# Kept sums stored by token tile, output channels regrouped for 2 KB reloads, and the second V weight quarter on ScalarE's DMA queue

## The chip, the cores and the metric

One core of one Trainium2 chip. The metric is device time in microseconds (us), and the granted clock of TensorE is 1.0 for nearly every run.

Engines in the profile: PE is TensorE's matmul part, PEld its weight loads, DVE VectorE, ACT ScalarE, POOL GpSimd, SP SyncE (which issues nearly all DMAs).

## The reference, cut to what matters

Two transformer-like layers, each an attention part A and a gated feed-forward part B, over 2048 tokens of 1024 channels. The attention looks at 8 earlier tokens at a distance of 2 (0, 2, ... 14 back), in 32 heads of 32 channels.

```python
def _A_ref(x, wqkv, wo):                 # H = 32, Dh = 32, W = 8, dil = 2
    q, k, v = ...(x @ wqkv)
    logits = einsum("bhsd,bhswd->bhsw", q, k at s - 2*w) * Dh**-0.5
    o = einsum("bhsw,bhswd->bhsd", softmax(logits, -1), v at s - 2*w)
    return o.reshape(B, S, D) @ wo
x = x + _A_ref(_layernorm(x), ...);  x = x + _B_ref(_layernorm(x), ...)   # twice
```

## The kernel before

The kernel works on blocks of 512 tokens (BLK), four tiles of 128 (TPB) each; two layers of four blocks make the numbers n = 0 to 7. VectorE multiplies q by the shifted k and sums over channel groups. What remains is S: 128 partitions (32 heads x 4 partial sums) by 8 window places by 512 tokens. S goes to DRAM and comes back with heads and token tiles on the partitions, for the softmax. (Block 0 alone sums over the heads' partitions with TensorE instead.) The attention output O goes to DRAM and comes back channel by channel as the stationary operand of the Wo matmul.

```python
s_d = [dram.tile([P, W, BLK], BF16, name=f"s_d{i}") for i in range(2)]
...
def store_s(n, half): ...
    sp_dma(s_d[n % 2][:, ws, :], att[n]["s"][:, ws, :])          # 4 KB runs
def load_s(n): ...
    for tq in range(TPB):
        src = bass.AP(tensor=sd.tensor, offset=sd.offset + tq * P,
                      ap=[[DG * W * BLK, H], [BLK, DG * W], [1, P]])   # 256-byte runs
        sp_dma(s4[32 * tq:32 * tq + 32, :, :, :].rearrange("p d w t -> p (d w) t"), src)
def load_o(n): ...
    for tq in range(TPB):
        src = bass.AP(..., ap=[[P, P], [P * P, KC], [1, P]])           # 256-byte runs
        sp_dma(oTa[:, :, tq, :], src)
```

The start is a hand-made pipeline. While the inputs arrive, 13 "scratch" matmuls on ones keep TensorE busy. x tile 0 is normalized by VectorE (`bn`, `aggr`, `apply`) with a power on GpSimd, transposed by TensorE, copied out of PSUM by ScalarE and VectorE, and multiplied by the first half of V's weights. Tile 1 follows. Its eight transposes (`turn`) are done in two groups of four, which lie in one PSUM tile.

```python
def load_x(b, tiles): ...   # tile 0: half on SyncE's queue, half on ScalarE's; tile 2: ScalarE's queue
load_x(0, range(TPB - 1)); ...
load_slab(("v0", 0), ...)   # V weights, quarters 1 and 2, both on SyncE's queue
load_x(0, [TPB - 1])
load_slab(("v0", 1), ...)   # quarters 3 and 4
load_slab(("qk01", "q", 0), ...)
...
scratch(13)
bn(0, 0); bn(0, 1); aggr(0)
act_square(2); act_mean(2)              # ScalarE, before its copies of tile 0
bn(1, 0); apply(0, 0); apply(0, 1); turn(0)
copy(0, "a", 0, 0, KC // 4); copy(0, "a", 0, KC // 4, KC // 2)
...
both = psum_l.tile([P, 2, KC, P], BF16, tag="L", name="tp_pair")   # tile 1: one PSUM tile
tps[t] = [both[:, h, 0:KC // 2, :] for h in range(2)]
...
def second(h): turn(1, (h,)); copy(1, "v", h); ...
def head():
    for kc in range(KC // 2):
        if kc == KC // 2 - 1: ln["second"](0)     # after 24 matmuls of tile 0
        for c in range(KC): prod(kc, c, 0, 1)
    ln["second"](1)
```

## Time and profile before

| | before |
|---|---|
| time, median of 3 | 1618.2 us (1617.9 to 1618.39) |
| span of the profiled run | 1616.4 us |
| PE busy | 1611.3 us |
| first V matmul / steady V products of tile 1 / first Q projection (chain) | 8.09 / 10.80 / 24.04 us |

From the page of the kernel before: busy time and share of PE, DMA packets by size, and two of the DMA issues (KB each, median us from issue to landing).

```profile
PE 1611.3 (100%) x7633; PEld 786.6 (49%) x7633; DVE 1137.1 (70%) x960; ACT 475.8 (29%) x968; POOL 180.4 (11%) x168
...
DMA packets 407448, 317.92 MB, mean 197 GB/s; under 512 B 166464, under 2 KB 387008, under 8 KB 406848
...
w_o<-in_A_wo_dram SPq DMA_DIRECT2D x16, 1024.0 KB, 7.0
oT<-o_d SPq DMA_DIRECT2D x32, 256.0 KB, 4.5
```

The S reloads from the list of DMAs:

```profile
s<-s_d SPq DMA_DIRECT2D x28, 256.0 KB, 6.1
```

All that PE ever waited for (total us, times, longest us):

```profile
PE scratch L132 <- DVE ones L310: 1.5, 1, 1.5
PE acc_v L132 <- ACT xnT_first L328: 0.4, 1, 0.4
```

The chain of work that ended last, at its start (start us, duration us, what):

```profile
5.45 1.16 ACT xn_first L328 x2
6.63 1.15 ACT xn_first L328 x2
7.78 0.27 ACT xnT_first L328
8.09 1.50 PE acc_v L132 x24
9.59 0.33 PE tp_pair L385 x4
9.94 0.43 DVE xnT_first L106
10.42 0.38 PE tp_pair L385 x4
10.80 3.53 PE acc_v L132 x48
...
24.04 2.16 PE acc_q L132 x10
```

How to read it: a DMA's landing is the moment at which its completion is seen, and the chain is followed back from the last instruction, at each step to what released it. A slab is a part of a weight matrix loaded by one call. PE waits 1.5 us for its first operand and 0.4 us for the first transposed copy, and never again. From 24.04 us on the chain is matmul after matmul, eight of 128x512 in 1.727 us. About 7332 of these, 56 half-wide ones and the 8 head-sum matmuls of block 0 (0.55 us) add up to 1582.6 + 6.1 + 0.55 = 1589.3 us, which is the whole way to the last matmul near 1613.3 us. Only the 24 us at the start can change, as long as nothing new makes PE wait later. In the chain the first matmul (8.09) hangs on ScalarE's copy, which stands behind the square and mean of x tile 2 (5.45 to 7.78).

### The profile page before, as it was taken

How to read it: one execution, taken by the hardware profiler on the slowest of the kernel's cores; microseconds unless marked ns; L12 is line 12 of the kernel's file. 1: busy time of each engine (PE TensorE's matmuls, PEld its weight loads, DVE VectorE, ACT ScalarE, POOL GpSimd, SP SyncE). 2: the span in 40 equal slices, each digit the busy share in tenths (PEclk: the TensorE clock that was granted, in tenths of full speed). 3: DMA queues.
4: the chain of work that ended last, by engine and by line, in shares of the span. 5: the costliest groups of instructions: out<-in, count | busy, mean ns of one | idle time of the engine just before them, and what ended most of it. 6: DMA issues, size and time to landing. Idle time of an engine off the chain costs nothing.

```text
span 1616.4 us, 18930 instructions
## 1 busy us (share of the span) xinstructions
PE 1611.3 (100%) x7633; PEld 786.6 (49%) x7633; DVE 1137.1 (70%) x960; ACT 475.8 (29%) x968; POOL 180.4 (11%) x168
## 2 busy tenths in 40 slices
PE   9999999999999999999999999999999999999999
PEld 6646544444444445444454444544445444444444
DVE  5999989996989698929489293893939939311211
ACT  5853312132116313603136031361313311131110
POOL 2400100010003002300053000530005100000000
PEclk9999999999999999999999999999999999999999
DMA  9868868697669766794847947479574794755452
GB/s 306 180 190 238 224 159 262 183 216 204 208 192 217 200 184 212 192 246 146 227 160 201 240 153 230 152 205 252 165 226 155 203 245 157 209 161 177 157 167 68
DMA packets 407448, 317.92 MB, mean 197 GB/s; under 512 B 166464, under 2 KB 387008, under 8 KB 406848
## 3 DMA queue, kind: packets, MB, share of 16 engines
q1 hardware_dynamic: 406784, 316.13, 69.9%
q8 instruction: 59, 0.97, 0.3%
q10 hardware_dynamic: 576, 0.59, 0.1%
q14 instruction: 29, 0.24, 0.0%
HBM read 266.29 MB, written 34.66 MB: 186 GB/s over the span
## 4 chain that ended last, share of the span: by engine, by line
PE 99%; DMA 0%; ACT 0%; DVE 0%; issue 0%; ACTq 0%; DVEq 0%
PE acc_u L132 24%; PE acc_g L132 24%; PE dacc L132 18%; PE acc_v L132 7%; PE acc_wo L132 7%; PE acc_k L132 7%; PE acc_q L132 7%; PE dacc_pair L132 6%; DMA x<-in_A_x_dram 0%; ACT xn_first L328 0%; PE tp_pair L385 0%; PE L L132 0%; DVE x L837 0%; DVE xnT_first L106 0%; ACTq L175 0%
## 5 line engine op out<-in xcount | busy, mean ns | idle before, releaser
L132 PE MATMUL acc_g<-xnT_b,w_g 128*128 128x512 bf16 x1792 | 423.3, 379 | 0.0
L132 PE MATMUL acc_u<-xnT_b,w_u 128*128 128x512 bf16 x1792 | 423.3, 379 | 0.0
L790 ACT ACTIVATE r<-acc_g 128x512 bf16<-128x512 f32 x224 | 133.5, 596 | 726.7 <-PE acc_g L132 701.6
L106 DVE TENSOR_TENSOR hT<-acc_u,r 128x512 bf16<-128x512 f32 x224 | 150.5, 685 | 240.7 <-PE acc_u L132 238.2
L132 PE MATMUL dacc<-w_d,hT 128*128 128x512 bf16 (+1 forms) x1400 | 301.9, 375 | 0.0
L132 PEld LDWEIGHTS <-hT 128*128 128x128 bf16 x1820 | 178.1, 98 | 208.9
L132 PEld LDWEIGHTS <-w_u 128*128 128x128 bf16 x1792 | 175.3, 98 | 211.5
L132 PEld LDWEIGHTS <-w_g 128*128 128x128 bf16 x1792 | 175.4, 98 | 211.4
L106 DVE TENSOR_TENSOR pv<-a,vhm 128x4096 bf16<-128x4096 bf16 x64 | 143.4, 2281 | 0.0
L837 DVE TENSOR_TENSOR x<-dacc,x 128x512 bf16<-128x512 f32 (+1 forms) x38 | 24.5, 672 | 154.2 <-PE dacc L132 154.2
L608 DVE TENSOR_TENSOR t<-q,k 128x2048 f32<-128x2048 bf16 x56 | 128.0, 2292 | 6.7 <-ACT k L543 4.6
L106 DVE TENSOR_TENSOR t<-q,k 128x2048 f32<-128x2048 bf16 x56 | 127.4, 2285 | 3.7 <-ACT k L543 2.6
L106 DVE TENSOR_TENSOR pv<-pv 128x1024 bf16<-128x1024 bf16 (+1 forms) x128 | 113.6, 947 | 0.0
L549 POOL COPY kh<-k 128x14 bf16<-128x14 bf16 x40 | 56.0, 1406 | 504.3 <-ACT k L543 504.3
L132 PE MATMUL acc_wo<-w_o,oT 128*128 128x512 bf16 x512 | 111.8, 379 | 0.0
L621 DVE TENSOR_TENSOR ac<-ac,t 128x2048 f32<-128x2048 f32 x48 | 109.6, 2284 | 0.3
L106 DVE TENSOR_TENSOR ac<-ac,t 128x2048 f32<-128x2048 f32 x48 | 109.5, 2282 | 0.0
L264 POOL TENSOR_TENSOR st_b<-st_b,neg_half 128x1 f32<-128x1 f32 x29 | 43.9, 1523 | 525.8 <-ACT st_b L263 525.7
L132 PE MATMUL dacc_pair<-w_d,hT 128*128 128x512 bf16 x420 | 95.9, 379 | 0.0
L132 PEld LDWEIGHTS <-oT 128*128 128x128 bf16 x512 | 50.0, 98 | 60.4
L259 ACT ACTIVATE xn_b<-x 128x1024 bf16<-128x1024 bf16 x29 | 30.3, 1045 | 129.1 <-DVE x L106 67.0
L446 ACT CAST vT<-acc_v 128x512 bf16<-128x512 f32 x56 | 32.8, 588 | 57.6 <-PE acc_v L132 56.6
(134 smaller groups left out, 1230.0 us busy)
## 6 DMA issues: line engine op xcount, KB each, us to landing
w_g<-in_B_W_gate_dram SPq DMA_DIRECT2D x56, 1024.0 KB, 7.4
w_u<-in_B_W_up_dram SPq DMA_DIRECT2D x56, 1024.0 KB, 5.5
w_d<-in_B_W_down_dram SPq DMA_DIRECT2D x48, 1024.0 KB, 5.7
w_o<-in_A_wo_dram SPq DMA_DIRECT2D x16, 1024.0 KB, 7.0
vhm<-v_d SPq DMA_DIRECT2D x32, 284.0 KB, 6.8
v_d<-vT SPq DMA_DIRECT2D x8, 1024.0 KB, 9.8
oT<-o_d SPq DMA_DIRECT2D x32, 256.0 KB, 4.5
w_d<-in_B_W_down_dram SPq DMA_DIRECT2D x16, 512.0 KB, 3.9
```

The lines of the kernel that those rows point to most:

```text
L106: tail_dve[0] = f(*args, **kwargs).ins
L132: tail_pe[0] = nc.tensor.matmul(*args, **kwargs).ins
L259: nc.scalar.activation(xn, xt[:], ACT.Square, accum_out=sq)
L264: nc.gpsimd.tensor_tensor(rstd, vpe, neg_half[:, 0:1], op=ALU.pow)
L446: tail_act[0] = nc.scalar.copy(st["vT"][:, c, :], acc[:]).ins
L549: nc.gpsimd.tensor_copy(khalo[n][:, c, :], k[:, BLK:BLK + HALO])
L608: nc.vector.tensor_tensor(t[:], i0, i1, op=ALU.mult)
L621: nc.vector.tensor_tensor(o, ac[:], t[:], op=ALU.add)
L790: tail_act[0] = nc.scalar.activation(rs[j][:], acc[:], ACT.Relu).ins
L837: run = dv if n < NB - 2 else (lambda f, *args, **kwargs: f(*args, **kwargs))
```

## The change

Intent: S is kept by token tile, so that a reload takes 2 KB runs; O is reloaded with eight neighbouring channels per partition, also in 2 KB runs, and Wo's rows are regrouped to match. At the start, ScalarE's copies come before its work on tile 2, tile 3's statistics move to VectorE, tile 1's first transposes come four matmuls later, and V's second weight quarter goes to ScalarE's DMA queue in place of x tile 2.

```diff
-    wo_v = A_wo.rearrange("(kc p) n -> p kc n", p=P)
+    wo_v = A_wo.rearrange("(p kc) n -> p kc n", kc=KC)
-    s_d = [dram.tile([P, W, BLK], BF16, name=f"s_d{i}") for i in range(2)]
+    s_d = [dram.tile([P, TPB, W, P], BF16, name=f"s_d{i}") for i in range(2)]
-            elif t == 2:
-                nc.scalar.dma_start(x_tiles[t][:], x_dram[t * P:(t + 1) * P, :])
-    load_x(0, range(TPB - 1))
+    load_x(0, [0, 1])
-                sp_dma(tv[:, rows, :], src[:, rows, :])
+                start = nc.scalar.dma_start if (key[1], i) == (0, 1) else sp_dma
+                start(tv[:, rows, :], src[:, rows, :])
-    load_x(0, [TPB - 1])
+    load_x(0, [2, 3])
-        act_square(2)
-        act_mean(2)
         bn(1, 0)
         ...
         copy(0, "a", 0, KC // 4, KC // 2)
+        act_square(2)
+        act_mean(2)
         ...                       # tile 3: bn and aggr on VectorE, after tile 1's copies
-                if kc == KC // 2 - 1:
-                    ln["second"](0)
                 for c in range(KC):
+                    if (kc, c) == (KC // 2 - 1, KC // 2):
+                        ln["second"](0)
-                       rhs=st["s"][:, WH * wh:WH * (wh + 1), tq * P:(tq + 1) * P],
+                       rhs=st["s"][:, tq, WH * wh:WH * (wh + 1), :],
-            o = st["s"][:, WH * h:WH * (h + 1), :] if c == KC - 1 else ac[:]
+            if c == KC - 1:
+                o = _ap(st["s"], WH * h * P, [[P, WH], [W * P, TPB], [1, P]])
-                              ap=[[DG * W * BLK, H], [BLK, DG * W], [1, P]])
+                              ap=[[DG * W * BLK, H], [W * BLK, DG], [1, W * P]])
-                              ap=[[P, P], [P * P, KC], [1, P]])
-                sp_dma(oTa[:, :, tq, :], src)
+                              ap=[[KC * P, P], [1, KC * P]])
+                sp_dma(oTa[:, tq, :, :].rearrange("p c t -> p (c t)"), src)
 ... (shapes and slices that follow from these left out)
```

More of the change, by code (lines that the diff above doesn't have):

```diff
@@ L408, in ln_first @@
         copy(0, "v", 1)
-        act_power(2)
         apply(1, 0)
@@ L414, in second @@
             turn(1, (h,))
+            copy(1, "v", h)
             if h == 0:
-                copy(1, "v", 0)
                 return
-            copy(1, "v", 1)
+            bn(3, 0)
+            act_power(2)
+            bn(3, 1)
+            aggr(3)
             apply(2)
-            act_square(3)
-            act_mean(3)
-            act_power(3)
             apply(3)
@@ L596, in f @@
                 if h == 0 and c == 0:
-                    st["s"] = big_tile([P, W, BLK], f"s_{n}")
+                    st["s"] = big_tile([P, TPB, W, P], f"s_{n}")
                 i0, i1 = qk_bcast(n, c, WH * h, WH)
@@ L616, in add @@
             ac, t = st["ac"], st.pop(("t", c))
-            o = st["s"][:, WH * h:WH * (h + 1), :] if c == KC - 1 else ac[:]
+            o, i0, i1 = ac[:], ac[:], t[:]
+            if c == KC - 1:
+                o = _ap(st["s"], WH * h * P, [[P, WH], [W * P, TPB], [1, P]])
+                i0, i1 = (i[:].rearrange("p w (q t) -> p w q t", t=P) for i in (ac, t))
             if n < NB:
-                dv(nc.vector.tensor_tensor, o, ac[:], t[:], op=ALU.add)
+                dv(nc.vector.tensor_tensor, o, i0, i1, op=ALU.add)
             else:
-                nc.vector.tensor_tensor(o, ac[:], t[:], op=ALU.add)
+                nc.vector.tensor_tensor(o, i0, i1, op=ALU.add)
         return [mult(h, c) for h in range(2) for c in range(KC)]
@@ L627, in f @@
             ws = slice(WH * half, WH * (half + 1))
-            sp_dma(s_d[n % 2][:, ws, :], att[n]["s"][:, ws, :])
+            sp_dma(s_d[n % 2][:, :, ws, :], att[n]["s"][:, :, ws, :])
         return f
@@ L635, in f @@
             for tq in range(TPB):
-                src = bass.AP(tensor=sd.tensor, offset=sd.offset + tq * P,
-                              ap=[[DG * W * BLK, H], [BLK, DG * W], [1, P]])
-                sp_dma(s4[32 * tq:32 * tq + 32, :, :, :].rearrange("p d w t -> p (d w) t"), src)
+                src = bass.AP(tensor=sd.tensor, offset=sd.offset + tq * W * P,
+                              ap=[[DG * W * BLK, H], [W * BLK, DG], [1, W * P]])
+                sp_dma(s4[32 * tq:32 * tq + 32, :, :, :].rearrange("p d w t -> p d (w t)"), src)
             att[n]["s4"] = s4
@@ L733, in f @@
             b = n % NB
-            oTa = big_tile([P, KC, TPB, P], f"oT_{n}")
+            oTa = big_tile([P, TPB, KC, P], f"oT_{n}")
             for tq in range(TPB):
                 src = bass.AP(tensor=o_d.tensor, offset=o_d[b * TPB + tq:b * TPB + tq + 1].offset,
-                              ap=[[P, P], [P * P, KC], [1, P]])
-                sp_dma(oTa[:, :, tq, :], src)
+                              ap=[[KC * P, P], [1, KC * P]])
+                sp_dma(oTa[:, tq, :, :].rearrange("p c t -> p (c t)"), src)
             att[n]["oT"] = oTa
@@ L755, in f @@
                         for c in range(KC):
-                            mm(accs[t, half][:], lhsT=st["oT"][:, c, t, :], rhs=slab[("o", n, half)][:, c, :],
+                            mm(accs[t, half][:], lhsT=st["oT"][:, t, c, :], rhs=slab[("o", n, half)][:, c, :],
                                start=(c == 0), stop=(c == KC - 1))
```

## The prediction

> **What bounds the kernel.** TensorE, almost without a gap. The page shows PE busy 1611.3 of 1616.4 us at granted clock 1.0. The Trainium skill, "Trainium Kernel Development and Optimization" (Performance Expectations), calls matmul busy time a bad metric because matmuls are pipelined, so I counted. In the chain of waits eight 128x512 matmuls take 1.727 us everywhere (216 ns each). From 24.04 us, where the first Q projection starts, to the last matmul near 1613.3 us there are about 7332 such matmuls, 56 half-wide ones and the 8 head-sum matmuls (0.55 us): 1582.6 + 6.1 + 0.55 = 1589.3 us, the whole stretch. No PE time is lost there. The list of PE waits agrees: 1.5 us for the ones tile and 0.4 us for the first transposed copy, nothing else. Only the first 24 and last 3 us can change, and the diff does not touch the tail.
>
> **Regrouping S and O.** Each S reload (28 issues of 256 KB, median 6.1 us to landing) and O reload (32 of 256 KB, 4.5 us) is cut into 256-byte runs. 4096 packets per block become 512: of 407448 packets about 48,000 go (25,000 for S, 29,000 for O, less 5,000 more on the S store, which goes from 4 KB to 1 KB runs). I expect landings roughly halved (estimate, from about 280 GB/s in the slices of an O reload against 380 to 400 in the 2 KB weight loads at the start). What waits for these: VectorE 2.2 us in all for S; PE never for O. Off the path, worth 0. Wo's rows are permuted to match, still 1 KB runs. The last add of S gets a four-level pattern; fp32 adds take 2.28 to 2.29 us whatever their layout (broadcast and shifted forms alike), so I expect 2.29 us still. It must: S of block 0 ends at 102.65 us and its head-sum matmuls run at 103.4.
>
> **The start.** Before: x tile 0 lands near 4.0 us; statistics, power and apply end near 6.9; transposes 6.97 to 7.69. ScalarE's copy waits behind square and mean of tile 2 (5.45 to 7.78), so the first V matmul starts at 8.09. After, the copies go first: start about 7.45, first matmul about 7.8, a gain of 0.3 us. But the next link eats it: tile 1's apply ends its first half at 9.41 (GpSimd power to 9.01), and 28 matmuls, four transposes, VectorE copy, four transposes give 7.8 + 28 x 0.0625 = 9.55, then about 0.9 us to the second transposes, about 10.4, against 10.42 before. The steady run begins at 10.8 in both. Risk: V's first quarter now shares bandwidth with the second one on ScalarE's queue; at the measured 390 GB/s[...] it lands near 7.5 instead of 6.8, just in time. Tiles 2 and 3 land near 8.2 and 8.8; apply of 2 ends near 13.2, of 3 near 14.7, before their transposes (14.2, 17.3).
>
> **Time.** 1618.2 - 0.1 = 1618.1 us, 8 in 10 within 1617.5 to 1618.6. Faster by over 2%: 0.003; within 2%: 0.994; slower: 0.003.
>
> **What would show it.** First V matmul near 7.8 us; first product of tile 1 near 10.8; Q projection near 24.0; the chain from there unchanged within 0.1 us; packets near 359,000; S and O landings near half; S add 2.29 us.
>
> **What would make it wrong.** V's quarter landing after 7.8 us; a slower patterned S add stalling the head sums at 103 us; tile 2's apply coming after 14.2 us; an O or S load colliding with a weight load so that PE waits.

## The result, and the profile after

| | before | after |
|---|---|---|
| time, median of 6 | 1618.42 us (1617.9 to 1619.06) | 1618.22 us (1618.09 to 1618.59) |
| span of the profiled run | 1616.4 us | 1616.1 us |
| chain: first V matmul / tile 1 steady / first Q | 8.09 / 10.80 / 24.04 | 7.55 / 10.52 / 23.76 us |
| DMA packets; of these under 512 B | 407,448; 166,464 | 359,064; 105,024 |

The ratio is 0.9999, 95% interval 0.9986 to 1.0012: the same. (Ratios are the mean time of one kernel's fast runs over that of the other's in the same rounds, so not quite the ratio of the medians quoted.)

The lines that answer to those of before. Page of the changed kernel:

```profile
PE 1607.6 (99%) x7584; PEld 786.4 (49%) x7633; DVE 1138.5 (70%) x962; ACT 473.5 (29%) x964; POOL 180.3 (11%) x168
...
DMA packets 359064, 317.92 MB, mean 197 GB/s; under 512 B 105024, under 2 KB 332736, under 8 KB 358464
...
w_o<-in_A_wo_dram SPq DMA_DIRECT2D x16, 1024.0 KB, 8.2
oT<-o_d SPq DMA_DIRECT2D x32, 256.0 KB, 3.4
```

PE's smaller busy time is no gain: the trace has 7584 of the 7633 matmul records, some are missing. The S reloads:

```profile
s<-s_d SPq DMA_DIRECT2D x28, 256.0 KB, 6.1
```

PE's waits:

```profile
PE scratch L132 <- DVE ones L309: 1.5, 1, 1.5
PE tp L384 <- DVE xn_first L106: 0.8, 1, 0.8
PE tp_pair L384 <- DVE xnT_first L106: 0.3, 1, 0.3
```

The start of the chain:

```profile
0.81 2.89 DMA x<-in_A_x_dram
...
6.24 0.41 DVE xn_first L106
6.69 0.41 PE tp L384 x4
7.13 0.38 ACT xnT_first L327
7.55 1.72 PE acc_v L132 x28
9.27 0.36 PE tp_pair L384 x4
9.66 0.44 DVE xnT_first L106
10.13 0.38 PE tp_pair L384 x4
10.52 3.53 PE acc_v L132 x48
...
23.76 2.37 PE acc_q L132 x11
```

Three things stand out. The DMA side changed as intended: 48,384 packets fewer, and the O reload lands in 3.4 us instead of 4.5. But the S reload takes 6.1 us as before, and Wo's loads take 8.2 us instead of 7.0. And the whole start sits 0.28 us earlier (10.52 against 10.80; 23.76 against 24.04). It is tempting to call this 0.28 us the gain of the new start. x tile 0 landed earlier by just that much, though: VectorE's first statistics began at 3.72 us against 4.00. Did the change do that?

My theory: the landing of x tile 0 is chance, and the new order gains nothing because the next link, tile 1's transposes, takes the gain. Rivals: the new queues bring tile 0 in earlier; the new order brings the 0.28 us; or the regrouping helps somewhere later. For the reloads, my theory was that they have slack everywhere.

### The profile page after: what moved, and what is told of

It reads as the page before. It is cut to its first block, busy times and chain, and to the rows that moved or that the text cites. A ratio compares the mean times of both kernels' runs of the same rounds, so it can differ in the third digit from the quotient of the medians.

```text
span 1616.1 us, 18879 instructions
## 1 busy us (share of the span) xinstructions
PE 1607.6 (99%) x7584; PEld 786.4 (49%) x7633; DVE 1138.5 (70%) x962; ACT 473.5 (29%) x964; POOL 180.3 (11%) x168
## 2 busy tenths in 40 slices
DMA packets 359064, 317.92 MB, mean 197 GB/s; under 512 B 105024, under 2 KB 332736, under 8 KB 358464
## 4 chain that ended last, share of the span: by engine, by line
PE 99%; issue 0%; DMA 0%; DVE 0%; POOL 0%; ACT 0%; DVEq 0%
PE acc_u L132 24%; PE acc_g L132 24%; PE dacc L132 18%; PE acc_v L132 7%; PE acc_k L132 7%; PE acc_q L132 7%; PE acc_wo L132 7%; PE dacc_pair L132 6%; DMA x<-in_A_x_dram 0%; PE tp_pair L384 0%; DVE bst L103 0%; DVE bst L106 0%; POOL rstd L327 0%; PE L L132 0%; DVE x L838 0%
```

## The experiments

Twelve runs were made (two of them repeat the unchanged kernels), all in the fast state (three had a single execution, whose state counts as unknown; their clock was 1.0). All were correct but one. Since times under 0.5 us cannot be told apart, the table shows the start of each trace: where tile 0's statistics began (x tile 0 had landed), tile 0's first transpose, the first V matmul, the steady V products of tile 1 and the first Q projection in the chain (us; the V products of "all three" from the timeline), beside the median time and the median of the kernel before of the same call. The expectations below partly quote the timeline, which puts the first Q matmul about 0.16 us sooner than the chain does (23.88 against 24.04 us before). In the rows with an own PSUM tile the chain gives the 48 products of tile 1 3.69 us instead of 3.53: add 0.16 us to "tile 1 steady" there before comparing it with the other rows, or compare the first Q projection.

| run | stats | transposes | first V | tile 1 steady | first Q | time | before |
|---|---|---|---|---|---|---|---|
| before | 4.00 | 6.97 | 8.09 | 10.80 | 24.04 | 1618.42 | |
| before, again | 3.71 | 6.68 | 7.53 | 10.51 | 23.75 | 1617.80 (1 run) | 1618.93 (1 run) |
| after | 3.72 | 6.69 | 7.55 | 10.52 | 23.76 | 1618.22 | 1618.42 |
| after, again | 3.62 | 7.05 | 7.90 | 10.87 | 24.11 | 1618.21 (1 run) | 1618.93 (1 run) |
| regrouping only | 3.60 | 7.04 | 8.11 | 10.73 | 23.97 | 1618.12 | 1618.06 |
| order only | 3.53 | 6.79 | 7.64 | 10.76 | 24.00 | 1618.15 | 1618.06 |
| queues only | 4.13 | 7.10 | 10.89 | 14.94 | 28.18 | 1622.94 | 1618.06 |
| own PSUM tile | 4.14 | 7.11 | 7.97 | 10.56 | 23.96 | 1618.24 | 1618.06 |
| own PSUM tile, 11 scratch | 3.63 | 6.60 | 8.29 | 10.76 | 24.16 | 1617.95 | 1618.45 |
| V quarter back on SyncE | 3.51 | 6.87 | 7.72 | 10.56 | 24.00 | 1618.58 | 1618.45 |
| all three | 3.90 | 6.87 | 7.84 | 10.57 | 24.50 | 1618.29 | 1618.18 |

### The same two kernels, profiled again

No edit. These were the last two runs, and they are told first because they settle the 0.28 us.

> The unchanged kernel before, profiled once more, to see how far the start of one and the same program scatters. In the first trace tile 0's statistics began at 4.00 us and the steady V products of tile 1 at about 10.8 us. If the 0.28 us between the two first traces is chance of the input loads: the statistics begin anywhere from 3.5 to 4.1 us here, and the first Q matmul starts from 23.6 to 24.0 us (first trace 23.88). If the old queues make it: 3.95 to 4.05 us again.

> The changed kernel, profiled once more. If the early landing in its first trace (statistics at 3.72 us, first Q matmul at 23.59 us) belongs to the change: 3.65 to 3.8 us and 23.5 to 23.7 us again. If it is chance: the statistics begin anywhere from 3.5 to 4.15 us and the first Q matmul anywhere from 23.5 to 24.0 us.

The two kernels changed places. The chain of the kernel before, second profile:

```profile
7.53 1.05 PE acc_v L132 x16
...
10.51 3.53 PE acc_v L132 x48
...
23.75 1.29 PE acc_q L132 x6
```

and of the changed kernel, second profile:

```profile
7.90 1.72 PE acc_v L132 x28
...
10.87 3.54 PE acc_v L132 x48
...
24.11 1.94 PE acc_q L132 x9
```

The kernel before now has its first Q projection at 23.75 us, the changed one at 24.11. The second pair of traces turned the 0.28 us round into 0.36 us the other way, so the first difference is scatter. (By the timeline the first Q matmul came at 23.59 and 23.95 us; the first lies at the edge of what I had written.) Two details follow. First, in its second trace the kernel before has its first V matmul at 7.53 us, as early as the changed kernel's, with the old order: x tile 2 had landed early enough for ScalarE to be through with it when tile 0's transposes were done. So the wait behind square and mean, which I had read from the first trace, is not a fixed property of that order. Second, the changed kernel's delay in its second trace has a name, in the timeline (last column: idle before it, and what ended that):

```profile
5.98 0.69 DVE L106 BATCH_NORM_STATS2 bst<-x 128x6 f32<-128x512 bf16 x1 [0.83 <-DMA x<-in_A_x_dram]
```

VectorE's third statistics instruction waits 0.83 us for x tile 1, and tile 0's apply stands behind it in VectorE's queue. Over all 14 traces, x tile 1 landed 3.4 to 4.7 us after its issue (mean 4.2) in the seven with V's quarter behind tile 0 on ScalarE's queue, and VectorE waited for it in four of them (0.16 to 0.83 us). In the seven others it landed in 3.0 to 3.9 us (mean 3.6), and VectorE never waited. The Trainium skill's page "DMA: Bandwidth & Descriptors" (section "Issuing engines are not separate DMA queues") says that DMAs of all issuing engines run interleaved on the same 16 DMA engines. These traces agree with that: with the moved quarter in flight beside it, x tile 1 comes later. x tile 0 itself began between 3.62 and 4.14 us with the moved quarter and between 3.51 and 4.00 without.

### The regrouping alone

```diff
 (only the hunks for wo_v, s_d, S, load_s, load_o and the Wo matmul; start as before)
```

> Only the regrouping of S, O and Wo, with the start as before. My theory (the reloads are off the critical path): time within 0.3 us of before, first V matmul at 8.1 us or 3.8 to 4.15 us after x tile 0's statistics begin, about 359,000 DMA packets, O landings near 3.4 us against 4.5, PE waits only at the start. Rival (the reloads have an edge somewhere in the attention stretch): PE waits in the middle vanish or the chain from the first Q projection to the end shortens by over 0.3 us.

Measured: ratio 1.0002 (0.9987 to 1.0017), packets 359,064, O landings 3.4 us, no PE wait after the start. The theory that the reloads are off the critical path holds for the time. The first V matmul came at 8.11 us, 4.51 us after the statistics began, later than I expected. The timeline shows why:

```profile
1.52 5.73 PE L132 MATMUL scratch<-ones 128*128 128x512 bf16 x13 [1.52 <-DVE ones L310]
7.04 0.82 PE L385 MATMUL tp<-ident,xn_first 128*128 128x128 bf16 x8
```

13 scratch matmuls took 5.73 us, until 7.25, and tile 0's transposes, whose data had been applied from 6.10 us on, queued behind them (7.04). In the 12 traces with 13 scratch matmuls these took from 4.33 to 5.73 us. The Trainium skill, "TensorE: Matmul & The Clock Gate" (Part 1), says that the array runs at half clock until a free-running activity window of about 3.4 us has seen it busy, so that the number of slow matmuls differs from run to run. The spacing here agrees: the slow ones come every 0.43 us, against 0.216 us later. So in such a trace an x tile 0 that lands early gains nothing, because the scratch work is not done.

### The order alone

```diff
 (only the hunks in the first layer norm and in head; queues and layout as before)
```

> Only the new order of ScalarE's and VectorE's work on the first block, old DMA queues, old layout. My theory (tile 1's link eats the gain): the first V matmul comes 0.25 to 0.35 us earlier, measured from the start of tile 0's statistics (3.8 us instead of 4.1), yet the second four transposes of tile 1 start 6.4 us after them as before; time within 0.2 us of before. Rival (the order brings the 0.28 us that the after trace showed): second transposes near 6.1 us after the start of the statistics. On x tile 0: if its landing near 3.7 us in the after trace came from the new queues, it lands near 4.0 here; if that was chance from run to run, it can be anything from 3.7 to 4.0.

Measured: ratio 1.0 (0.9983 to 1.0017). The second transposes came 10.38 - 3.53 = 6.85 us after the statistics, not 6.4: neither number that I had written; the first V matmul came 7.64 - 3.53 = 4.11 us after them, not 3.8. The chain names a new link, just ahead of the last 12 matmuls of tile 0 before the transposes:

```profile
2.20 6.55 DMA w_v<-in_A_wqkv_dram
```

x tile 0 had landed at 3.53 us, so the matmuls were ready early, and V's second quarter landed only at 8.75 us. The scratch matmuls (until 6.95 us) had already taken 0.3 us from the same chain. The order gained nothing in this trace: the links around it decided.

This trace also holds the only PE delay after the start in the traces with single reloads. It has the old layout. In block 0 a w_u load, issued behind the S reloads at 240.26 us, landed at 247.44, and PE's weight load waited for it (timeline):

```profile
247.48 1.41 PEld L132 LDWEIGHTS <-w_u 128*128 128x128 bf16 x8 [0.58 <-DMA w_u<-in_B_W_up_dram]
```

PE lost 0.27 us (from the first Q projection to the one near 605 us in the chain it took 581.08 us, 580.81 in the kernel before). In the three other old-layout traces with single reloads the same load landed only 0.04 to 0.18 us before its first weight load, in the eight with the new layout 0.24 to 1.32 us before it. So at this spot the old reloads had almost no slack, and the regrouping bought some; it is too little to show in the time.

### The queues alone

```diff
 (only the hunks in load_x, load_slab and the two load_x calls; order as before)
```

> Only the new DMA queues (tile 2 of x behind V's first quarter, second V quarter on ScalarE's queue), old order. My theory: ScalarE's square and mean of tile 2 now wait for its landing near 8.1 us and stand before the first copy, so the first V matmul starts near 10.7 us instead of 8.1, the second transposes near 13.1 instead of 10.4, and the time is 2 to 3.5 us longer than before. Rival (the queues alone are harmless or bring the gain): time within 0.4 us of before. x tile 0's statistics start near 3.7 us if the queues cause the early landing.

Measured: 1622.94 us against 1618.06, ratio 1.0031 (1.0016 to 1.0046), slower by 4.9 us. The direction and the first matmul (10.89 us, expected 10.7) are as the theory said: with x tile 2 behind V's quarters, ScalarE's square and mean of it wait for its landing at 8.24 us and hold up the first copy. x tile 0's statistics began at 4.13 us, so the new queues do not by themselves bring it in early.

```profile
PE acc_v L132 <- ACT xnT_first L327: 3.1, 1, 3.1
```

The size was off, because the clock came in. The windows of this run (PE, PEld, DVE, ACT and POOL busy, then granted clock, DMA share, GB/s):

```profile
8.00:11.00 3.00, 0.10 (x2) 0.10 (x2) 0.88 (x4) 2.71 (x6) 0.82 (x3) 0.96 1.05 392
11.00:13.00 2.00, 2.00 (x21) 2.00 (x21) 0.49 (x2) 1.97 (x4) 0.81 (x2) 0.50 1.05 387
```

PE idled for 3.07 us, and the clock it was granted fell to 0.50; the next matmuls ran at half speed (the first 24 took 2.72 us instead of 1.50), and the second transposes came at 14.61 us instead of the expected 13.1. The Trainium skill, "TensorE: Matmul & The Clock Gate", warns of PE-idle gaps over about 3 us ("Why this matters for your kernels"); this gap of 3.07 us agrees. So the order hunks gained nothing by themselves, but the new queues need them.

### Tile 1's second transposes in a PSUM tile of their own

```diff
 (changed kernel)
                 tps[t] = [both[:, h, 0:KC // 2, :] for h in range(2)]
+                if t == 1:
+                    tps[t][1] = psum.tile([P, KC // 2, P], BF16, tag="acc", name="tp1b")[:]
```

> The changed kernel, with the second four transposes of x tile 1 in a PSUM tile of their own, so that they need not wait for VectorE's copy of the first four. My theory (this wait is the link that eats the gain): PE's 0.3 us wait for the copy disappears, the second transposes start right after four matmuls, about 6.05 us after the start of tile 0's statistics instead of 6.41, and the steady run of tile 1 begins 0.25 to 0.4 us earlier; time 0.2 to 0.4 us shorter than the changed kernel, hardly clear of the noise. Rival (tile 1's apply is the limit): the second transposes stay at 6.4 us after the statistics begin.

```profile
7.97 1.72 PE acc_v L132 x28
...
10.08 0.44 DVE xnT_first L106
...
10.56 3.69 PE acc_v L132 x48
```

The transposes' wait for VectorE's copy, 0.3 us in the changed kernel, is gone: by the timeline the second transposes start 10.10 - 4.14 = 5.96 us after the statistics, against 10.13 - 3.72 = 6.41 in the changed kernel. Only half of that arrives, because tile 1's products now stand behind VectorE's copy of the first four (10.08 to 10.52). The first Q projection comes 23.96 - 4.14 = 19.82 us after the statistics, against 23.76 - 3.72 = 20.04: a gain of 0.22 us, just under the 0.25 to 0.4 that I had written. The link is real, and another one stands close behind it. The time does not show it (1618.24 against 1618.06, ratio 1.0002, 0.9987 to 1.0017): tile 0's statistics began only at 4.14 us in this trace, which more than gave the 0.22 us back, and the four runs scatter by 1.3 us in any case.

### ... and 11 scratch matmuls

```diff
-        scratch(13)
+        scratch(11)
```

> The changed kernel with the second transposes of x tile 1 in a PSUM tile of their own and 11 scratch matmuls instead of 13. My theory after the first four runs: the start is held by several nearly equal links (landing of x tile 0, which varied from 3.5 to 4.1 us; scratch matmuls that run to 7.2 us while the clock is still cold; V's quarters; the PSUM tile). Scratch ends near 6.2 us even at 0.43 us each, so tile 0's transposes start 0.42 to 0.48 us after the apply begins, whatever the clock; the first Q projection starts 19.75 to 19.85 us after tile 0's statistics begin (20.04 in both kernels), so between 23.3 and 24.0 us. Time within 0.5 us of before: not to be told from noise. Rival (11 are too few and the clock falls back): granted clock under 1.0 between 6 and 12 us and a first Q projection after 24.3 us.

Measured: 1617.95 us against 1618.45, ratio 0.9996 (0.9984 to 1.0009): not to be told from 1. Tile 0's transposes did start 6.60 - 6.13 = 0.47 us after the apply, and 28 matmuls of tile 0 took 1.74 us (62 ns each, as 24 in 1.50 us before), so 11 were enough here. But the first Q projection came at 24.16 us, outside what I expected, for a new reason:

```profile
PE acc_v L132 <- DMA w_v<-in_A_wqkv_dram: 1.0, 1, 1.0
```

V's first quarter landed only at 8.24 us, 6.5 us after its issue, past the 7.8 us that the prediction had named as its risk.

### V's second quarter back on SyncE's queue

```diff
 (changed kernel)
-                start = nc.scalar.dma_start if (key[1], i) == (0, 1) else sp_dma
-                start(tv[:, rows, :], src[:, rows, :])
+                sp_dma(tv[:, rows, :], src[:, rows, :])
```

> The changed kernel, with V's second weight quarter on SyncE's queue again (right behind the first), so that ScalarE's queue holds only half of x tile 0. Theory (the move to ScalarE's queue buys nothing because first and second quarter then share bandwidth): the first quarter lands about 0.7 us earlier than in the changed kernel (near 6.5 us) and no weight load waits for it; the second lands near 7.6 us, before it is needed; the second transposes of tile 1 start 6.4 us after tile 0's statistics begin, as in the changed kernel; time within 0.3 us of before. Rival (the move is needed): weight loads wait for the second quarter, by over 0.2 us, and the first Q projection comes over 0.2 us later relative to the statistics. For x tile 0: if a V quarter right behind it on ScalarE's queue slows it, it lands by 3.7 us here, and near 4.1 us in the other runs of this set that keep the new queue.

Measured: ratio 1.0001 (0.9988 to 1.0015). No wait for either of the first two quarters in PE's list, and x tile 1 landed in 3.0 us, the fastest of all. But the first quarter landed at 1.72 + 5.4 = 7.1 us, not 6.5, and the second transposes came 10.18 - 3.51 = 6.67 us after the statistics: the scratch matmuls (5.51 us, until 7.03) held tile 0's transposes. A later V quarter also held a weight load for 0.3 us at 12.59 us, so the first Q projection came 20.49 us after the statistics (20.04 and 20.49 in the two traces of the changed kernel). In the time, the move of the quarter buys nothing measurable, and undoing it does not either.

### All three

```diff
 (own PSUM tile, scratch(11), V's second quarter on SyncE's queue)
```

> The changed kernel with all three links loosened: second transposes of x tile 1 in a PSUM tile of their own, 11 scratch matmuls, V's second quarter back on SyncE's queue behind the first. In the run with 11 scratch matmuls alone TensorE waited 1.0 us for V's first quarter (landed 8.3 us); with the quarter on SyncE's queue no such wait was there. My theory (several nearly equal links, so that loosening one shows the next): no wait for w_v; first V matmul 3.7 to 3.9 us after tile 0's statistics begin, first Q projection 19.65 to 19.85 us after them, so near 23.3 us if they begin at 3.55 and near 23.9 if at 4.1 (before: 24.04). Time 0.3 to 0.8 us shorter than before, at or under the noise. Rival (another link I have not seen): first Q projection at 24.0 us again although the statistics begin by 3.7.

Measured: 1618.29 against 1618.18, ratio 0.9999 (0.9987 to 1.0012). My expectation missed: the first Q projection came at 24.50 us, the latest of all but the run with the queues alone. The chain:

```profile
4.41 8.63 DMA w_v<-in_A_wqkv_dram
13.09 1.70 PE acc_v L132 x14
```

A later V quarter landed at 13.04 us, and PE waited for it after tile 1 had long begun (there were two shorter waits of weight loads for the quarters before it). In this run the DMA engines moved 251 GB/s between 4 and 6 us, and in the one with the quarter back on SyncE's queue 288; the first traces of before and after moved 392 and 398. The order-only run, with the old queues, had 284 in the same stretch, and the second trace of the kernel before 313. All four slow stretches are among the seven traces with both of V's first two quarters on SyncE's queue (the other three: 371 to 392); the seven with the second quarter on ScalarE's queue moved 363 to 404. That speaks for a part of the queues in it, but with single traces of each kernel it is not shown, and what makes a stretch slow stays open. In the traces at full rate the engines are full: share 1.05, 392 GB/s from 4 to 13 us in the kernel before. x (1 MB) and V (2 MB) must come through that, whatever the order.

### Every reload twice, on the kernel before and on the changed one

```diff
 (load_s and load_o, once on the kernel before, once on the changed kernel)
-            for tq in range(TPB):
+            for tq in list(range(TPB)) * 2:
```

> The kernel before, with every S and O reload issued twice into the same tile (the second set waits for the first), 61,440 packets of 256 bytes more: the opposite of the change, about 1.2 times as large. My theory (the reloads have slack everywhere): no PE wait after the start, first Q projection to last matmul unchanged within 0.2 us, time within 0.5 us of before; at most one wait near a reload, under 2 us. Rival (they are on the edge and the regrouping buys safety): PE waits for w_g, w_u or oT appear, and the time grows by over 3 us.

> The changed kernel with every S and O reload issued twice, as the kernel before was in the run that came out 18 us slower: the same doubled work in 2 KB runs. Theory (the regrouping buys margin: four S reloads took SyncE's queue 2.5 to 3 us instead of 4.4 to 5.7): 3 to 9 us slower than the changed kernel, a wait for w_o in block 0 of 1 to 4 us instead of 6.2, one for w_u under 1 us. Rival (the wait of the second set for the first, not the run length, made the 18 us): 13 to 19 us slower here too.

The first was my worst miss: 1636.62 us against 1618.45, ratio 1.0107 (1.0091 to 1.0122), slower by 18.2 us, where I had expected under 0.5. PE's waits for weights after the start (a third, of 6.6 us in eight pieces, was for VectorE's gate product):

```profile
PE acc_wo L132 <- DMA w_o<-in_A_wo_dram: 6.7, 2, 6.2
...
PE acc_u L132 <- DMA w_u<-in_B_W_up_dram: 2.8, 1, 2.8
```

So the reloads are off the path, but not far off. In block 0 the four O reloads hold SyncE's queue, and Wo's second slab is issued behind them: at 153.56 us in the kernel before, landing 6.6 us later near 160.1; its matmuls start at 159.21 + 1.73 = 160.94. That is 0.8 us of slack, and the w_u load of the order-only section has less. With doubled reloads it was issued at 158.87, and PE waited 6.2 us.

The changed kernel with the same doubling took 1624.06 us against 1618.18, ratio 1.0038 (1.0023 to 1.0053), slower by 5.9 us, within the 3 to 9 that I had written (the wait for w_u, 1.1 us, is just over the "under 1 us"):

```profile
PE acc_wo L132 <- DMA w_o<-in_A_wo_dram: 2.4, 1, 2.4
...
PE acc_u L132 <- DMA w_u<-in_B_W_up_dram: 1.1, 1, 1.1
```

Doubled, 2 KB runs cost a third of what 256-byte runs cost (5.9 against 18.2 us), though in both the second set has to wait for the first; the rival, that this wait alone made the 18 us, falls. So the regrouping does take work from SyncE's queue and the DMA engines: four S reloads near 1314 us occupied SyncE's queue for 2.96 us instead of 5.73 (3.48 instead of 5.16 in the second traces), and from 1315 to 1321 us the engines moved 237 GB/s instead of 173 (210 instead of 171). This is worth time where reloads are on the path, as in the doubled runs, and nothing measurable here.

### Wo's rows in the old order

```diff
 (changed kernel; the result is wrong on purpose)
-    wo_v = A_wo.rearrange("(p kc) n -> p kc n", kc=KC)
+    wo_v = A_wo.rearrange("(kc p) n -> p kc n", p=P)
```

> The changed kernel with Wo's rows loaded in their old order (row kc x 128 + p to partition p), which gives a wrong result on purpose. It tells why Wo's loads land in 8.2 us with the change and in 7.0 before. If the new row order (eight neighbouring rows per partition) is the cause: 7.0 to 7.3 us again. If it is what runs beside them (they are issued sooner after the O reload): 8.0 to 8.3 us still. Time within 0.5 us of before in both cases.

```profile
w_o<-in_A_wo_dram SPq DMA_DIRECT2D x16, 1024.0 KB, 7.2
```

Wo's 16 loads landed in 7.2 us (median), against 8.2 with the regrouped rows: the row order is the cause. The other traces agree: 6.9 to 7.3 us in the five with the old rows, 7.7 to 8.3 in the eight with the new ones. Both orders read 1 KB runs; the new one reads a run of every 2 KB from eight neighbouring rows for one partition. Why that is slower no run shows. It matters for the slack: in the changed kernel Wo's second slab of block 0 is issued at 151.29, 2.3 us sooner than before, but lands 8.6 us later near 159.9, needed at 158.93 + 1.73 = 160.66. Again 0.7 to 0.8 us of slack: with single reloads the row order has eaten at this spot what the shorter runs gave (with old rows it landed near 151.33 + 7.3 = 158.6).

## Why the prediction was right or wrong, point by point

- **PE bounds the kernel and only the start can move: right.** No trace of the two kernels has a PE wait after the start, and all correct variants with more than one run, but for the queues alone and the doubled reloads, have medians within 0.5 us of the kernel before. (The single runs of the last pair lie 0.7 and 1.1 us under theirs, which is inside the scatter of one run.)
- **The time, 1618.1 us, same: right** (1618.22, ratio 0.9999).
- **Packets near 359,000: right** (359,064). **S add still 2.29 us: right**; the four-level pattern took 2.29 us in all 16 adds, and the head sums at 103.1 us did not stall. Tiles 2 and 3 were applied by 13.19 and 14.18 us, before their transposes at 13.89 and 16.98, as predicted.
- **"I expect landings roughly halved": wrong.** O went from 4.5 to 3.4 us, S stayed at 6.1 in the first pair; over all single-reload traces it went from 6.1 to 6.5 us (four with the old layout) to 5.5 to 6.1 (eight with the new). The estimate took the bandwidth of a reload for its landing time. My reading, which no run isolates: four S reloads are issued one behind the other and share the engines with each other and with weight loads; issued sooner, they queue longer. The time on SyncE's queue fell more clearly, from 5.73 to 2.96 us near 1314 us, but only from 3.35 to 2.47 near 386 us. I also missed that Wo's loads would slow by 1.2 us.
- **"Off the path, worth 0": right, but with less behind it than it seemed.** That PE waits for nothing says nothing about how much more would fit: doubling the reloads cost 18.2 us, with the longest single waits for Wo (0.8 us of slack) and w_u. The closest spot found, the w_u load of block 0, had 0.04 to 0.18 us in three old-layout traces and was late in the fourth, where it cost PE 0.27 us: the risk named in the prediction, an S load colliding with a weight load, was nearer than the first pair of traces showed.
- **"The copies go first: ... a gain of 0.3 us": wrong as a step.** It was read from one trace in which x tile 2 landed late. In the second trace of the same kernel the first V matmul came at 7.53 us, 3.82 us after the statistics, without any change; in the first trace of the changed kernel it was 3.83.
- **"But the next link eats it": right in kind, and too simple.** The sum held in the first trace: the second transposes came 10.13 - 3.72 = 6.41 us after the statistics, predicted 10.4 - 4.0 = 6.4, and 6.42 before; in the second trace of the changed kernel it was 6.87. The shared PSUM tile is one such link (0.22 us when loosened). The runs showed at least four more of about the same length: x tile 0's landing (3.5 to 4.1 us), the scratch matmuls at half clock (4.3 to 5.7 us), x tile 1's landing, V's quarters. Whatever is shortened, another one takes over.
- **"Just in time" for V's first quarter: right.** In the changed kernel a weight load waited for it until 7.41 us (predicted landing 7.5). In the run with 11 scratch matmuls it landed at 8.24, and PE waited 1.0 us: the named risk is real, and that it did not strike in the two traces of the changed kernel is in part luck.

What stays open: why the input loads ran at 251 to 313 GB/s in some starts, and why Wo's regrouped rows load more slowly. No version was found that beats the kernel before by more than the noise; the nearest (own PSUM tile, 11 scratch matmuls) has a ratio of 0.9996 with an interval that holds 1.

## What to carry to other kernels

When a tuned start is held by several links of nearly equal length, one trace shows only which was longest that time: profile the same kernel twice before explaining 0.3 us by an edit, and expect single repairs to show nothing. Compare intervals from a common event (here tile 0's statistics) to one that all versions reach in the same way (the first Q projection): a piece in between can be counted differently. A load that nothing waits for is worth nothing to speed up, but measure its slack by doubling it rather than inferring it from missing waits. A layout change that shortens one DMA's runs can lengthen another's (here Wo's rows): compare the landings of everything that it touches.

## What the Trainium skill lacked or had wrong

- "DMA: Bandwidth & Descriptors" (Specifications) gives 512 bytes as the least size for line rate. That did not tell the landing time here: S reloads in 2 KB runs landed in 5.5 to 6.1 us, hardly sooner than with 256 bytes (6.1 to 6.5), and their stretch moved 237 GB/s (173 before), while weight and x loads with 2 KB rows moved 392 GB/s at the start.
- The same page lacks the order of rows among equal runs at distances as small as here (its one entry on the distance between rows is for large powers of two): Wo's 1 MB in 1 KB runs landed in 8.2 us with eight neighbouring rows per partition and in 7.2 us with rows 128 apart.
- "TensorE: Matmul & The Clock Gate" (Part 1) is right that the warm-up differs from run to run, but does not say that work can queue behind warm-up matmuls. Here the same 13 warm-up matmuls took 4.33 to 5.73 us, and in three traces the first real work queued behind them for 0.3 to 0.5 us.
- I found no page that gives the scatter of the first loads of a kernel: the same first 128 KB (half of x tile 0) became usable between 3.51 and 4.14 us after the start, over 14 traces.
